# First chunk's attention units scheduled by priority, weight loads behind its stores, and a weight split with three VectorE operations and one more on ScalarE

## The chip, the cores and the metric

The kernel runs on one core of a Trainium2 chip. The metric is the time of one execution on the device, in microseconds (us). Three runs of the kernel before took 1007.69, 1010.55 and 1011.11 us; the median is 1010.55.

## The reference

Attention with a sliding window of 32 positions and 32 global tokens per batch, then a feed-forward layer with a residual. There are 8 batches, 8 heads, 512 local positions, 32 global ones and a head size of 64; all is float32.

```
s_ll = where(|i - j| <= 32, scale * q_l @ k_l.T, -1e9)      # local rows
s_l  = concat([scale * q_l @ k_g.T, s_ll]);  out_l = softmax(s_l) @ concat([v_g, v_l])
out_g = softmax(scale * q_g @ concat([k_g, k_l]).T) @ concat([v_g, v_l])
x   = concat([out_g, out_l])  as (8, 576, 512)
xn  = (x - mean) / sqrt(var + 1e-6) * g_ln
out = x + relu(xn @ w_ch1) @ w_ch2                          # 512 -> 2048 -> 512
```

## The kernel before

**Units and chunks.** A `Local` unit is one batch, one pair of heads and 256 positions. Its `scores` (L249) are TensorE's score matmuls (L262), VectorE's minimum of each row with the mask added (L275, four per unit) and ScalarE's exponential (L285, four). `transposes` (L294) turns the probabilities, for the first 16 units on TensorE (L299) with a copy `pt` on ScalarE (L301). `values` (L309) are the value matmuls (L316), a reciprocal of the sums (L326 on GpSimd, L327) and x on VectorE (L328). After the four units of a half, `finish` stores x to DRAM (L342, two stores on SP's queue) and `norm` takes its statistics (L189, L191 on VectorE, L193 and L194 on GpSimd) and normalises: by ScalarE (L202), or, for the last half of the first chunk, by VectorE into a new tile (L207). `transpose_chunk` (L484) turns x into the feed-forward's operand: a transpose on TensorE (L492), its high part `xh` on ScalarE (L504) and the rest `xl` on VectorE (L505).

A chunk is 512 rows. There are eight chunks of eight units each and one of the global rows. `ffn` runs a chunk through 16 slices of the weights: `mm1` (L531, 12 matmuls of 512 columns), ScalarE's `hh` (L539), VectorE's `hl` (L540) and `mm2` (L550, 12 matmuls, one slice behind). The units of the next chunk are dealt out among the slices.

**Weights.** Each slice arrives as 1024 packed 64-bit words per partition (`raw`, loaded at L165, 1 MB). In the first chunk `split_weights` (L133) makes a high and a low float32r part of each: ScalarE's L140, VectorE's L142 and L143, L145 and L146, ScalarE's cast L150, VectorE's L152. L145 and L146 are the last readers of `raw`. The buffers of raw words borrow the places of late weight slices (`RAWS`, L27): four for the first eight loads, then fewer, so a load waits until an earlier slice has been split. `tmp` has two buffers.

**Order.** Each engine runs its instructions in one order, and an instruction that waits holds what stands behind it. The block at L685 to L726 handles the first chunk's eight units (`need[0]` is 8, `HP` is 4). It runs under `manual_schedule` for SP, TensorE, VectorE and ScalarE: on these engines the order is that of the Python code. The code deals out one step of a weight split between the steps of the units from the fourth on (`SPLIT_FROM`). Loads of weights stand among those of the units (L690, L691). From L733 on TensorE alone has the written order; for the other engines a scheduler orders by its own estimate of times and by priority (`hurry` is `tc.high_priority()`).

Of the kernel before, what the change touches and what calls it, by code (L numbers as in the profile page):

```python
# [11 lines left out]
I32 = mybir.dt.int32  # L12
I16 = mybir.dt.int16
U16 = mybir.dt.uint16
# [3 lines left out]
ALU = mybir.AluOpType  # L18
# [8 lines left out]
RAWS = ("w15", "w14", "w13", "ob", "w15", "w14", "w13", "ob") + ("w15", "w14", "ob") * 2 + ("w15", "ob")  # L27
UNITS = ("w5", "w6", "w7", "w8", "w9", "w10", "w11", "w12")


SPLIT_AHEAD = 3
LOADS_AHEAD = 2
SPLIT_FROM = 3

ON_PE = 16

# [12 lines left out]
def attention_ffn_kernel(  # L49
# [33 lines left out]
    def f32(ap):  # L83
        return ap.bitcast(F32)
# [48 lines left out]
    def split_weights(ap, raw, hi, lo):  # L133

        third = raw.bitcast(U16).rearrange("p (n t) -> p n t", t=4)[:, :, 1]
        top = raw.bitcast(I32).rearrange("p (n t) -> p n t", t=2)[:, :, 1]
        tmp = ap.tile([P, KT * P + DM], F32, name="tmp", bufs=2)
        itmp = tmp.bitcast(I32)
        last = tmp.bitcast(U16).rearrange("p (n t) -> p n t", t=2)[:, :, 0]
        nc.scalar.activation(tmp, f32(top), AF.Abs, scale=REBIAS)  # L140
        yield
        nc.vector.tensor_scalar(tmp, tmp, HUGE, None, ALU.min)  # L142
        nc.vector.tensor_scalar(itmp, itmp, 3, None, ALU.logical_shift_left)  # L143
        yield
        nc.vector.scalar_tensor_tensor(last, third, THIRD, last, ALU.mult, ALU.add)  # L145
        nc.vector.scalar_tensor_tensor(  # L146
            itmp, top, SIGN, itmp, ALU.bitwise_and, ALU.bitwise_or
        )
        yield
        nc.scalar.copy(hi, tmp)  # L150
        yield
        nc.vector.tensor_tensor(lo, tmp, f32(hi), op=ALU.subtract)  # L152
# [67 lines left out]
    class Local:  # L220
# [88 lines left out]
        def values(self):  # L309
            b, hp, half = self.at  # L310
            pv = self.bank(3, "pv")
            for h in range(2):
                for qb in range(2):
                    for g in range(4):
                        gp = slice(g * WIN, (g + 1) * WIN)
                        nc.tensor.matmul(  # L316
                            pv[gp, qb * P + h * D:qb * P + h * D + D],
                            self.pt[:, 2 * h + qb, gp],
                            self.v[:, 4 * qb + g, h * D:(h + 1) * D],
                            start=True,  # L320
                            stop=True,
                            tile_position=(0, g * WIN),
                            skip_group_check=True,
                        )
            ri = small.tile([P, 4], F32, name="ri")
            nc.gpsimd.tensor_scalar(ri, self.sm, SUM_EPS, None, ALU.add)  # L326
            nc.vector.reciprocal(ri, ri)  # L327
            nc.vector.tensor_tensor(  # L328
                self.x[:, :, hp * P:(hp + 1) * P].rearrange("p q (h d) -> p q h d", h=2),
                pv[:, :256].rearrange("p (q h d) -> p q h d", q=2, h=2),  # L330
                ri.rearrange("p (h q) -> p q h", h=2).unsqueeze(3).to_broadcast([P, 2, 2, D]),
                op=ALU.mult,
            )
            if not self.alone and self.next and self.next.next:
                self.next.next.load()
# [346 lines left out]

    ET = mybir.EngineType
    xt = []
    with tc.manual_schedule(engines={ET.SP, ET.PE, ET.DVE, ET.Activation}):  # L685
        begin(0)
        nc.sync.dma_start(g_sb, g_ln.rearrange("(t p) o -> p (t o)", p=P))
        for n in range(2, need[0]):
            units[n].load()
            load_weights_to((n - 1) // 2)  # L690
        load_weights_to(4)  # L691
        units[need[0]].load()
        units[need[0] + 1].load()
        splits = weights_to(SPLIT_AHEAD)
        scores = [u.scores() for u in units[:need[0]]]
        moves = {}
        after = {}
        next(scores[0])
        for n in range(need[0] + 2):
            if n < need[0]:  # L700
                for _ in scores[n]:
                    pass
            if n + 1 < need[0]:
                next(scores[n + 1])
            if 0 <= n - 1 < need[0]:
                moves[n - 1] = units[n - 1].transposes()
                next(moves[n - 1])
            if n > SPLIT_FROM:
                next(splits, None)
            if 0 <= n - 1 < need[0]:  # L710
                for _ in moves[n - 1]:
                    pass
            if n >= 2:
                after[n - 2] = values(units[n - 2])
            if n >= SPLIT_FROM:
                next(splits, None)
            if n == HP + 2:
                for _ in after[HP - 1]:
                    pass
            if n == HP + 3:  # L720
                for _ in transpose_chunk(tiles_of(ready[0][:1]), xt, 0, 4):
                    pass
        for _ in after[need[0] - 1]:
            pass
        for _ in transpose_chunk(tiles_of([units[need[0] - 1].xn]), xt, 2, 4):
            pass  # L726
    for _ in splits:
        pass
    ready.pop(0)
    traced["units"] = need[0]  # L730
    for c, chunk in enumerate(chunks):
# [119 lines left out]
```

## Time and profile before

| | |
|---|---|
| median of three runs | 1010.55 us |
| the profiled execution | 1013.72 us |
| its span | 1011.9 us |
| busy: TensorE, VectorE, ScalarE, GpSimd | 950.4, 588.1, 299.0, 44.5 us |
| chain of waits, by engine | TensorE 85%, VectorE 7%, ScalarE 2%, DMA 2%, issue 2% |

Times in a timeline count from the start of the span. The profile gives each group of instructions the line that recorded it, so the two kernels have different line numbers at the top: a split's L140, L142, L143, L145 are now L138, L139, L141, L142, while L146 to L152 and all from there up to L681 are the same in both. A matmul's listed duration includes its passage through the array, so start to start is the time it takes from the next. Durations on VectorE and ScalarE overlap in the same way by a little.

### The profile page before, as it was taken

The page shows a single profiled execution, that of the slowest core. Times are in us where ns is not written, and L with a number is a line of the kernel's source. Part 1 is how long each engine was busy: PE and PEld are TensorE (multiplying, and loading weights), DVE is VectorE, ACT ScalarE, POOL GpSimd, SP SyncE. Part 2 cuts the span into 40 slices and gives each one's busy share as a digit, 9 for nine tenths or more (in the row PEclk, how much of TensorE's full clock was granted, in tenths as well). Part 3 has the DMA queues.
Part 4 walks back from the last instruction along what each step waited for, and adds up shares of the span by engine and source line. Part 5 has one row for each costly group of instructions (what it writes and reads, how often), then busy time and mean ns, then how long its engine had stood idle before and what let it go on. Part 6 is the DMA issues. An engine that isn't in the chain of part 4 may idle for free.

```text
span 1011.9 us, 21071 instructions
## 1 busy us (share of the span) xinstructions
PE 950.4 (94%) x8616; PEld 719.4 (71%) x8616; DVE 588.1 (58%) x1889; ACT 299.0 (30%) x826; POOL 44.5 (4%) x150
## 2 busy tenths in 40 slices
PE   5429999999999999999999999999999989989997
PEld 3216777677777777777777777777777766766796
DVE  2699952567667666666667666767666632222311
ACT  5545542322232223222222223222212232222210
POOL 3010000000000000000000000000000000000000
PEclk9859999999999999999999999999999999999999
DMA  9645542232233222322232224212322344543110
GB/s 363 254 146 198 202 162 90 84 105 90 70 131 113 90 71 91 123 90 100 80 131 91 70 90 154 91 70 90 119 81 87 110 159 147 186 140 133 32 42 21
DMA packets 31872, 118.80 MB, mean 117 GB/s; under 512 B 4256, under 2 KB 6304, under 8 KB 27680
## 3 DMA queue, kind: packets, MB, share of 16 engines
q1 hardware_dynamic: 31776, 117.46, 33.8%
q8 instruction: 68, 1.11, 0.4%
q14 instruction: 28, 0.23, 0.1%
HBM read 99.62 MB, written 17.83 MB: 116 GB/s over the span
## 4 chain that ended last, share of the span: by engine, by line
PE 85%; DVE 7%; ACT 2%; DMA 2%; issue 2%; POOL 1%; SPq 0%; ACTq 0%; DVEq 0%
PE acc L550 36%; PE ph L531 36%; PE sc L262 5%; PE pv L316 3%; DVE tmp L145 2%; PE t L492 1%; PE pv L419 1%; DVE w L152 1%; DVE tmp L146 1%; ACT p L285 1%; PE sc L371 1%; DMA u<-in_eu 1%; PE tp L299 1%; DVE hl L540 1%; PE t L407 1%
## 5 line engine op out<-in xcount | busy, mean ns | idle before, releaser
L550 PE MATMUL acc<-w,hh 128*128 128x512 f32 x1088 | 344.3, 398 | 0.0
L531 PE MATMUL ph<-xh,w 128*128 128x512 f32 (+1 forms) x1216 | 311.8, 383 | 0.0
L307 DVE STREAM_TRANSPOSE pt<-p 32x128 f32<-32x128 f32 x768 | 232.6, 303 | 62.5 <-ACT p L285 50.4
L531 PEld LDWEIGHTS ph<-xh,w 128*128 128x128 f32 x1216 | 214.0, 189 | 49.8 <-issue 3.1
L550 PEld LDWEIGHTS acc<-w,hh 128*128 128x128 f32 x1088 | 206.7, 190 | 44.8
L550 PE MATMUL acc<-w,hl 128*128 128x512 f32 x544 | 226.3, 416 | 2.2 <-DVE hl L540 2.2
L540 DVE SCALAR_TENSOR_TENSOR hl<-ph,hh 128x512 fp32r<-128x512 f32 (+1 forms) x144 | 94.3, 656 | 171.0 <-ACT hh L539 169.5
L539 ACT ACTIVATE hh<-ph 128x512 fp32r<-128x512 f32 (+1 forms) x144 | 82.2, 571 | 362.8 <-PE ph L531 361.7
L285 ACT ACTIVATE p<-p,mn 128x128 f32<-128x128 f32 x256 | 99.8, 391 | 197.9 <-DVE mn L275 197.9
L531 PE MATMUL ph<-xl,w 128*128 128x512 f32 x512 | 143.7, 402 | 0.0
L550 PEld LDWEIGHTS acc<-w,hl 128*128 128x128 f32 x544 | 102.9, 189 | 31.9 <-issue 7.0
L531 PEld LDWEIGHTS ph<-xl,w 128*128 128x128 f32 x512 | 94.3, 189 | 27.9 <-issue 6.9
L275 DVE CUSTOM_DVE_ANT_0 p<-sc,mask 128x128 f32<-128x128 f32 x256 | 58.7, 286 | 45.7 <-PE sc L262 40.0
L262 PE MATMUL sc<-u 64*32 64x128 f32 x2048 | 57.5, 295 | 23.1 <-DMA u<-in_eu 8.5
L262 PEld LDWEIGHTS sc<-u 64*32 64x32 f32 x2048 | 31.9, 112 | 52.4 <-issue 35.9
L328 DVE TENSOR_TENSOR x<-pv,ri 128x256 f32<-128x256 f32 x64 | 26.9, 420 | 60.0 <-PE pv L316 59.8
L316 PEld LDWEIGHTS pv<-u,pt 128*32 128x32 f32 x2048 | 33.9, 116 | 22.6 <-issue 21.4
L285 ACT ACTIVATION_READ_ACCUMULATOR p<-p,mn 128x1 f32 x256 | 47.8, 187 | 0.0
L316 PE MATMUL pv<-u,pt 128*32 128x64 f32 x2048 | 44.5, 232 | 0.0
L492 PE MATMUL t<-ident,x 128*128 128x128 f32 x136 | 23.1, 291 | 21.1 <-DVE x L207 13.2
L326 POOL TENSOR_SCALAR ri<-sm 128x4 f32<-128x4 f32 x64 | 16.6, 259 | 589.1 <-ACT p L285 588.6
L202 ACT ACTIVATE x<-x,rs 128x512 f32<-128x512 f32 x32 | 24.8, 810 | 43.0 <-DMA xs<-x 42.9
(58 smaller groups left out, 440.3 us busy)
## 6 DMA issues: line engine op xcount, KB each, us to landing
u<-in_eu SPq DMA_DIRECT2D x63, 848.0 KB, 4.7
raw<-in_wd SPq DMA_DIRECT2D x16, 1024.0 KB, 6.1
gk<-in_gk SPq DMA_DIRECT2D x8, 1088.0 KB, 5.1
xs<-x SPq DMA_DIRECT2D x32, 256.0 KB, 5.6
ob<-xs SPq DMA_DIRECT2D x32, 256.0 KB, 3.9
out<-ob SPq DMA_DIRECT2D x32, 256.0 KB, 2.1
gv<-in_gv SPq DMA_DIRECT2D x8, 1024.0 KB, 5.0
u<-in_eu SPq DMA_DIRECT2D x1, 512.0 KB, 3.7
```

The costliest lines, as they stand in the source:

```text
L202: nc.scalar.activation(x[:, j, :], x[:, j, :], AF.Identity, bias=rs[:, 1, j:j + 1], scale=rs[:, 0, j:j + 1],)
L262: nc.tensor.matmul(sc[h][gp, qb * P:(qb + 1) * P], self.e[hd, w * WIN:(w + 1) * WIN], self.e[hd, k0 * WIN:(k0 + 4) * WIN], start=True, sto ...
L275: nc.vector.tensor_tensor_reduce(out=self.p[:, c], in0=sc[h][:, qb * P:(qb + 1) * P], in1=masks[half, qb], scale=-QSCALE, scalar=BIG, op0= ...
L285: nc.scalar.activation(self.p[:, c], self.p[:, c], AF.Exp, bias=mn[:, c:c + 1], scale=-1.0, accum_out=self.sm[:, c:c + 1],)
L307: nc.vector.transpose(out=self.pt[rp, :, gp], in_=self.p[gp, :, rp])
L316: nc.tensor.matmul(pv[gp, qb * P + h * D:qb * P + h * D + D], self.pt[:, 2 * h + qb, gp], self.v[:, 4 * qb + g, h * D:(h + 1) * D], start= ...
L328: nc.vector.tensor_tensor(self.x[:, :, hp * P:(hp + 1) * P].rearrange("p q (h d) -> p q h d", h=2), pv[:, :256].rearrange("p (q h d) -> p ...
L492: nc.tensor.transpose(t[:, j * P:(j + 1) * P], xn[j][:, kt * P:(kt + 1) * P], ident)
L531: nc.tensor.matmul(ph[:, :n], w[:, kt, :], xx[kt][:, :n], start=(i == 0), stop=(i == 3 * KT - 1),)
L539: nc.scalar.activation(hh[:, :n], ph[:, :n], AF.Relu)
L540: nc.vector.scalar_tensor_tensor(hl[:, :n], ph[:, :n], 0.0, f32(hh[:, :n]), ALU.max, ALU.subtract)
L550: nc.tensor.matmul(acc[t], a[:, ts], w, start=(f == 0 and i == 0), stop=(f == NF - 1 and i == 2),)
```

## The change

It has three parts. In the split, VectorE's L145 goes: ScalarE scales the 16-bit field itself (new L139, into the low word of `raw`, in place) and VectorE's shift takes it in by an or (new L142, in place of L143). The first chunk's block keeps only SP in written order; the units' code stands under `hurry(True)`, and the splits come after it, without priority. And SP's order is written anew: in front of the units only slice 0 is loaded; slice 1 and two units of the next chunk are loaded behind the stores of the first half, slices 2 and 3 behind those of the second.

```
@@ -27,10 +27,8 @@
 RAWS = ("w15", "w14", "w13", "ob", "w15", "w14", "w13", "ob") + ("w15", "w14", "ob") * 2 + ("w15", "ob")
 UNITS = ("w5", "w6", "w7", "w8", "w9", "w10", "w11", "w12")
 
-
 SPLIT_AHEAD = 3
 LOADS_AHEAD = 2
-SPLIT_FROM = 3
 
 ON_PE = 16
 
@@ -136,13 +134,15 @@
         top = raw.bitcast(I32).rearrange("p (n t) -> p n t", t=2)[:, :, 1]
         tmp = ap.tile([P, KT * P + DM], F32, name="tmp", bufs=2)
         itmp = tmp.bitcast(I32)
-        last = tmp.bitcast(U16).rearrange("p (n t) -> p n t", t=2)[:, :, 0]
+        last = raw.bitcast(I32).rearrange("p (n t) -> p n t", t=2)[:, :, 0]
         nc.scalar.activation(tmp, f32(top), AF.Abs, scale=REBIAS)
+        nc.scalar.activation(last, third, AF.Copy, scale=THIRD)
         yield
         nc.vector.tensor_scalar(tmp, tmp, HUGE, None, ALU.min)
-        nc.vector.tensor_scalar(itmp, itmp, 3, None, ALU.logical_shift_left)
+        nc.vector.scalar_tensor_tensor(
+            itmp, itmp, 3, last, ALU.logical_shift_left, ALU.bitwise_or
+        )
         yield
-        nc.vector.scalar_tensor_tensor(last, third, THIRD, last, ALU.mult, ALU.add)
         nc.vector.scalar_tensor_tensor(
             itmp, top, SIGN, itmp, ALU.bitwise_and, ALU.bitwise_or
         )
@@ -682,50 +682,46 @@
 
     ET = mybir.EngineType
     xt = []
-    with tc.manual_schedule(engines={ET.SP, ET.PE, ET.DVE, ET.Activation}):
+    with tc.manual_schedule(engines={ET.SP}):
         begin(0)
         nc.sync.dma_start(g_sb, g_ln.rearrange("(t p) o -> p (t o)", p=P))
         for n in range(2, need[0]):
             units[n].load()
-            load_weights_to((n - 1) // 2)
-        load_weights_to(4)
-        units[need[0]].load()
-        units[need[0] + 1].load()
-        splits = weights_to(SPLIT_AHEAD)
-        scores = [u.scores() for u in units[:need[0]]]
-        moves = {}
-        after = {}
-        next(scores[0])
-        for n in range(need[0] + 2):
-            if n < need[0]:
-                for _ in scores[n]:
-                    pass
-            if n + 1 < need[0]:
-                next(scores[n + 1])
-            if 0 <= n - 1 < need[0]:
-                moves[n - 1] = units[n - 1].transposes()
-                next(moves[n - 1])
-            if n > SPLIT_FROM:
-                next(splits, None)
-            if 0 <= n - 1 < need[0]:
-                for _ in moves[n - 1]:
-                    pass
-            if n >= 2:
-                after[n - 2] = values(units[n - 2])
-            if n >= SPLIT_FROM:
-                next(splits, None)
-            if n == HP + 2:
-                for _ in after[HP - 1]:
-                    pass
-            if n == HP + 3:
-                for _ in transpose_chunk(tiles_of(ready[0][:1]), xt, 0, 4):
-                    pass
-        for _ in after[need[0] - 1]:
+            if n == 3:
+                load_weights_to(1)
+        with hurry(True):
+            scores = [u.scores() for u in units[:need[0]]]
+            after = {}
+            next(scores[0])
+            for n in range(need[0] + 2):
+                if n < need[0]:
+                    for _ in scores[n]:
+                        pass
+                if n + 1 < need[0]:
+                    next(scores[n + 1])
+                if 0 <= n - 1 < need[0]:
+                    for _ in units[n - 1].transposes():
+                        pass
+                if n >= 2:
+                    after[n - 2] = values(units[n - 2])
+
+                if n == HP + 1:
+                    load_weights_to(2)
+                    units[need[0]].load()
+                    units[need[0] + 1].load()
+                if n == HP + 2:
+                    for _ in after[HP - 1]:
+                        pass
+                if n == HP + 3:
+                    for _ in transpose_chunk(tiles_of(ready[0][:1]), xt, 0, 4):
+                        pass
+            load_weights_to(4)
+            for _ in after[need[0] - 1]:
+                pass
+            for _ in transpose_chunk(tiles_of([units[need[0] - 1].xn]), xt, 2, 4):
+                pass
+        for _ in weights_to(SPLIT_AHEAD):
             pass
-        for _ in transpose_chunk(tiles_of([units[need[0] - 1].xn]), xt, 2, 4):
-            pass
-    for _ in splits:
-        pass
     ready.pop(0)
     traced["units"] = need[0]
     for c, chunk in enumerate(chunks):
```

VectorE's row shows where the first split stands among the units. `mask_114` and `mask_122` mark the minima of the units of the second half, 4 to 7; `x` and `ri` belong to the unit named by its place. Before, from the middle of the first split:

```order
L142 TENSOR_SCALAR tmp<-tmp 128x1024
L143 TENSOR_SCALAR tmp<-tmp 128x1024
L327 RECIPROCAL ri<-ri 128x4
L328 TENSOR_TENSOR x<-pv,ri 128x2x128
L145 SCALAR_TENSOR_TENSOR tmp<-raw,tmp 128x1024
L146 SCALAR_TENSOR_TENSOR tmp<-raw,tmp 128x1024
L275 ISA p,mn<-sc,mask_114 128x128
L275 ISA mn 128x1
```

And now, the same stretch:

```order
L142 SCALAR_TENSOR_TENSOR tmp<-tmp,raw 128x1024
L328 TENSOR_TENSOR x<-pv,ri 128x2x128
L146 SCALAR_TENSOR_TENSOR tmp<-raw,tmp 128x1024
L327 RECIPROCAL ri<-ri 128x4
L152 TENSOR_TENSOR w<-tmp,w 128x1024
L275 ISA p,mn<-sc,mask_114 128x128
L275 ISA mn 128x1
L275 ISA p,mn<-sc,mask_122 128x128
```

Before, the split's L142 to L146 stood behind the minima of unit 4 and ahead of those of unit 5, with L152 later. Now the whole split stands ahead of the minima of unit 4, and no other split follows before unit 7's.

SP's row shows the loads (`u` of a unit, `raw` of a slice) and stores (`xs`) of the first chunk. Before:

```order
L245 DMA u<-in_eu 128x1696 x2
L165 DMA raw<-in_wd 128x1024
L245 DMA u<-in_eu 128x1696 x2
L165 DMA raw<-in_wd 128x1024
L245 DMA u<-in_eu 128x1696 x2
L165 DMA raw<-in_wd 128x1024 x2
L245 DMA u<-in_eu 128x1696 x2
L165 DMA raw<-in_wd 128x1024
L342 DMA xs<-x 128x512 x2
L165 DMA raw<-in_wd 128x1024 x3
L342 DMA xs<-x 128x512 x2
```

And now:

```order
L245 DMA u<-in_eu 128x1696 x2
L165 DMA raw<-in_wd 128x1024
L245 DMA u<-in_eu 128x1696 x4
L165 DMA raw<-in_wd 128x1024
L342 DMA xs<-x 128x512 x2
L165 DMA raw<-in_wd 128x1024
L245 DMA u<-in_eu 128x1696 x2
L165 DMA raw<-in_wd 128x1024
L342 DMA xs<-x 128x512 x2
L165 DMA raw<-in_wd 128x1024 x5
```

The first `raw` behind the four units is that of the fifth slice, which waits for the first split; those of the second, third and fourth slice moved behind stores that wait for x.

ScalarE's row shows the end of the first chunk's units, from the last unit's `pt` to the last `xh`, the operand's second half. Before:

```order
L301 COPY pt<-tp 128x512
L150 CAST w<-tmp 128x1024
L140 ACTIVATE tmp<-raw 128x1024
L150 CAST w<-tmp 128x1024
L140 ACTIVATE tmp<-raw 128x1024
L150 CAST w<-tmp 128x1024
L504 ACTIVATE xh_618<-t,g_sb 128x256 x2
L140 ACTIVATE tmp<-raw 128x1024
L504 ACTIVATE xh_630<-t,g_sb 128x256 x2
```

And now:

```order
L301 COPY pt<-tp 128x512
L139 ACTIVATE raw<-raw 128x1024
L504 ACTIVATE xh_593<-t,g_sb 128x256 x2
L138 ACTIVATE tmp<-raw 128x1024
L139 ACTIVATE raw<-raw 128x1024
L504 ACTIVATE xh_605<-t,g_sb 128x256 x2
L138 ACTIVATE tmp<-raw 128x1024
L139 ACTIVATE raw<-raw 128x1024
L150 CAST w<-tmp 128x1024
```

Casts (L150) went to later places, and the two operations on a raw slice (L138 and L139, here of the third and then the fourth slice) stand ahead of and behind the last `xh`.

## Rows read from the trace of the kernel before

**Rows 1.** The page's busy times: us (share of the span) and instructions.
```profile
PE 950.4 (94%) x8616; PEld 719.4 (71%) x8616; DVE 588.1 (58%) x1889; ACT 299.0 (30%) x826; POOL 44.5 (4%) x150
```

**Rows 2.** Windows: length; busy us of each engine; PEclk; DMA share; GB/s.
```profile
0.00:5.00 5.00, 1.11 (x32) 0.66 (x32) 0.00 (x0) 1.49 (x2) 4.06 (x24) 1.00 0.65 232
5.00:10.00 5.00, 1.23 (x32) 0.81 (x32) 1.84 (x15) 2.24 (x11) 3.90 (x19) 1.00 0.83 308
10.00:15.00 5.00, 4.12 (x72) 3.05 (x72) 1.14 (x11) 2.97 (x15) 0.22 (x1) 1.00 1.01 427
```

**Rows 3.** Timeline of TensorE: start, us, line, operation [idle before <- releaser].
```profile
17.43 1.57 PE L262 MATMUL sc<-u 64*32 64x128 f32 x32 [1.01 <-DVE mn L275]
18.93 1.11 PE L299 MATMUL tp<-ident,p 128*128 128x128 f32 x4
19.98 1.08 PE L316 MATMUL pv<-u,pt 128*32 128x64 f32 x32
...
67.76 1.27 PE L492 MATMUL t<-ident,x 128*128 128x128 f32 x4 [13.19 <-DVE x L207]
...
75.99 2.07 PE L531 MATMUL ph<-xh,w 128*128 128x512 f32 x4
...
100.27 0.67 PE L262 MATMUL sc<-u 64*32 64x128 f32 x32
...
189.62 1.20 PE L531 MATMUL ph<-xh,w 128*128 128x512 f32 x4
```

**Rows 4.** Timeline of VectorE, around the splits and the second statistics.
```profile
28.57 0.28 DVE L275 CUSTOM_DVE_ANT_0 p<-sc,mask 128x128 f32<-128x128 f32 x1
...
35.98 0.16 DVE L196 SCALAR_TENSOR_TENSOR rs<-mv,rs 128x2 f32<-128x2 f32 x1 [1.15 <-POOL rs L194]
...
57.60 1.23 DVE L152 TENSOR_TENSOR w<-tmp,w 128x1024 fp32r<-128x1024 f32 x1
58.73 1.24 DVE L146 SCALAR_TENSOR_TENSOR tmp<-raw,tmp 128x1024 int32<-128x1024 int32 x1
...
60.66 0.41 DVE L328 TENSOR_TENSOR x<-pv,ri 128x256 f32<-128x256 f32 x1
61.00 0.68 DVE L143 TENSOR_SCALAR tmp<-tmp 128x1024 int32<-128x1024 int32 x1
61.60 1.28 DVE L189 BATCH_NORM_STATS2 st<-x 128x6 f32<-128x512 f32 x2
62.79 1.28 DVE L145 SCALAR_TENSOR_TENSOR tmp<-raw,tmp 128x1024 uint16<-128x1024 uint16 x1
...
67.07 1.00 DVE L207 TENSOR_SCALAR x<-x,mv,rs 128x512 f32<-128x512 f32 x2 [0.63 <-POOL rs L194]
...
70.33 0.86 DVE L505 SCALAR_TENSOR_TENSOR xl<-t,g_sb,xh 128x256 fp32r<-128x256 f32 x2
```

**Rows 5.** Timeline of ScalarE.
```profile
40.93 1.52 ACT L202 ACTIVATE x<-x,rs 128x512 f32<-128x512 f32 x2
...
44.55 0.40 ACT L285 ACTIVATE p<-p,mn 128x128 f32<-128x128 f32 x1 [2.10 <-DVE mn L275]
...
46.10 1.03 ACT L150 CAST w<-tmp 128x1024 fp32r<-128x1024 f32 x1
47.04 0.57 ACT L301 COPY pt<-tp 128x512 f32<-128x512 f32 x1
47.52 1.15 ACT L140 ACTIVATE tmp<-raw 128x1024 f32<-128x1024 f32 x1
48.56 0.82 ACT L504 ACTIVATE xh<-t,g_sb 128x256 fp32r<-128x256 f32 x2
...
128.21 1.14 ACT L140 ACTIVATE tmp<-raw 128x1024 f32<-128x1024 f32 x1 [5.32 <-DMA raw<-in_wd]
```

**Rows 6.** SP's timeline; then DMA issues of 40 to 140 us: KB, us to landing.
```profile
33.32 1.56 SPq L342 DMA_DIRECT2D xs<-x  x2
...
raw<-in_wd SPq DMA_DIRECT2D x11, 1024.0 KB, 4.8
```

## Prediction, as put on record before the run

> **What bounds the kernel now.** I read the page first: TensorE is busy for 94% of the span [rows 1]. Then the windows and TensorE's timeline, to find where it is not at work. The first feed-forward matmul starts at 75.99 us, and the one that opens the second chunk at 189.62 [rows 3]; behind that the chain of waits is TensorE's nearly throughout. So the end moves by what moves TensorE through the first chunk: A, the time until the first feed-forward matmul, and B, the 113.6 us from there to 189.62.
>
> In A nothing is full. TensorE's last long wait before it, 13.19 us, is for VectorE's normalised tile (L207) of the second half [rows 3]; VectorE was at weight splits between the units' small operations, as at 57.60 to 62.79 [rows 4]. The eight units' own work is short, so A is a chain of waits and an order question. The clock: the window of 10 to 15 us reads 1.00 [rows 2], but 32 score matmuls take 1.57 us at 17.43 and 0.67 at 100.27 [rows 3]. I take the durations: 1.2 GHz in the early stretch, 2.4 GHz later.
>
> **Prices.** On VectorE and ScalarE listed durations overlap the next by about 0.09 us (57.60 + 1.23 against 58.73), so I take that off. VectorE [rows 4]: row minima of a unit 0.84 (four of 0.21), x 0.34, two statistics 1.19, L143 0.60, L145 1.18, L146 1.14, L152 1.13, two normalisations (L207) 1.0, two xl 0.8. ScalarE [rows 5]: four exponentials 1.55, the pt copy 0.48, L140 1.04, the cast L150 0.94, two xh 0.73, two L202 1.43. TensorE at the low level [rows 3]: scores 1.5, transposes 1.05, values 1.06. A reciprocal, a pair of aggregates or a hand-over between engines is put at 0.1.
>
> **The split.** Before, VectorE works 0.60 + 0.60 + 1.18 + 1.14 + 1.13 = 4.65 us on one slice. L145 goes; L143 becomes an operation on two tensors. No row shows that one: at least the 0.60 of L143, at most the 1.18 of L145; I take L146's 1.14, which reads the same kinds. New: 0.60 + 1.14 + 1.14 + 1.13 = 4.0, so 0.65 less (0.6 to 1.2). ScalarE gains L139 with 16-bit input: not below the cast's 0.94, not above the 1.18 that VectorE needs for these operands; I take L140's 1.04, so its slice costs 1.04 + 1.04 + 0.94 = 3.0. Over 16 slices VectorE gives up 10 us and ScalarE takes 17, but neither is on the path once TensorE is fed (B, below).
>
> **A: the order.** Before, VectorE ends five splits in A and is in the sixth, the first two between the units' steps. Now it ends one ahead of unit 4's minima, one behind unit 7's transposes, and part of two more at the end. I walk the new order, each engine in its row; SP's and ScalarE's orders are the two that new waits come from, GpSimd's changes only among masks and small additions.
> - To 17.0. Loads decide, as before. The first slice's raw stands behind four units' loads: 4.5 MB, which the 232, 308 and 427 GB/s of the first windows [rows 2] deliver by 14.3. ScalarE has some 0.6 of unit 2's exponentials and a copy ahead then, and goes on with L138 and L139: 17.0.
> - To 21.8. L142 1.14, x 0.34, L146 1.14, ScalarE's cast 0.94, L152 1.13, hand-overs 0.1: the split is done at 21.8. Scores of unit 4 were there at 18.6, so this first split costs the units 3.2. Minima 22.6, exponentials 23.7, copy 24.1.
> - To 28.5. ScalarE's next instruction is L139 of the fifth slice, whose load was issued when L146 freed its buffer (19.7) and stands behind units 4 to 7: 9.0 MB, at 425 GB/s landed at 25.0. It ends at 26.1, 2.0 late. Unit 5's exponentials end at 27.7; TensorE meanwhile does scores 6, and x of unit 3 is written at 28.5.
> - To 45.0. Statistics to 29.8, the hand-over to GpSimd and back 1.15 [rows 4], L202 to 32.6, unit 7's exponentials 34.2, a copy 34.7. Slice 1's load is issued behind two stores of x, 1.56 of issue [rows 6], at 30.2. A load issued alone lands in 4.8 [rows 6], with the stores' 0.5 MB in front (1.2 at 425 GB/s) 6.0: 36.2. L138 and L139 38.3, L142 39.4, x 39.8, xl 40.6; two transposes and xh 41.5, xl 42.0, unit 7's transposes 43.1, copy 43.6, values and x 45.0.
> - To 57.5. Two chains start from that x. One: statistics and aggregates 46.4, GpSimd 47.5, L207, transposes, xh: 50.0. The other: two stores 1.6, slice 2's load 5.4 (half the stores' 1.2 added): 52.0. On ScalarE L138 and L139 of slice 2 stand ahead of the last two xh: 54.1, xh 54.9, VectorE's L142 55.2, xl 56.0; unit 8's scores need the banks that this frees: 57.5.
>
> That makes the first feed-forward matmul 57.5; hand-overs that I dropped are put at 0.5: 58.0. A is shorter by 76.0 - 58.0 = 18.0. About 2 of what remains is the load behind the stores. The bounds of the two unknown prices move A by -1.6 to +0.1 (three L142 on the path) and by -0.4 to +0.6 (four L139).
>
> **B: is it still fed?** From unit 8's scores on TensorE's order is the same as before. At the start of B it has two slices split and a third under way, where before five were and a sixth under way. VectorE has 14 left: 14 x 4.0 + 16 hl of 0.6 + 8 units of 1.3 = 76 us, less than the 113.6 of B (before 10 x 4.65 + 9.6 + 10.4 = 67). ScalarE's 17 more lie beside these matmuls too. ScalarE has 3.0 + 0.5 + half a unit (1.0) = 4.5 a slice against TensorE's 113.6 / 16 = 7.1. But L139 of a later slice stands ahead of nearer casts and relus, and ScalarE waits in order for its load: walked through, that holds it 0.4 to 1.3 us a slice, and once (the tenth load) TensorE stands 2.2. Before has stalls of its own in B, about as much. I put B at no change, bounded by -3 and +5. SP's later stores stand ahead of the last load, which is needed 20 us later: nothing.
>
> **Sum.** The profiled execution is 1013.72 us, 1.8 around its span; less 18.0 makes 995.7. The median of the runs shown is 1010.55, 3.2 below the profiled one, so I expect 992.5.
>
> **Rivals.**
> 1. *TensorE wakes in the units.* In my walk it works from 10.9 to 21.1 almost without a gap, where before it was busy 4.12 of 5 us and stayed low [rows 2, 3]. At 2.4 GHz scores, transposes and values go from 3.6 to 1.6 a unit. Along the chain some four such steps of 0.5 to 1.0 and the last scores (0.9) come out, 4 us: 988. Against: the chain is held by ScalarE and loads, and narrow matmuls did not lift the clock before. The Trainium skill (TensorE: Matmul & The Clock Gate, Part 1) says half rate is the default and sustained activity releases it. By that rule this rival holds; the trace so far, with the score rows, speaks for the low level.
> 2. *The units come out slower than walked.* The loads that ScalarE waits for in A (first, second, third and fifth slice) each land later, 1.5 to 2.5 us, because unit loads share the engines; A ends at 66: 8 to 10 us gained, 1001. For it: ScalarE once stood 5.32 for a load [rows 5]. Against: later loads were issued into a quieter queue.
> 3. *Slower.* ScalarE's L139 waits in B become the bound. A slice has 7.1 - 4.5 = 2.6 us to spare; to lose the 18 won, 14 slices must each take 2.6 + 18 / 14 = 3.9 of waiting. If every load held ScalarE for its 4.8, a slice would be 9.3: 14 x 2.2 = 31 lost, less 18: 1023. Against: the loads are issued three slices ahead.
> 4. *The order does not matter:* VectorE's postponed splits (four more of 4.0 at the start of B) hold TensorE by just what A gave, 16 to 18: 1010.
>
> **Chances.** Forecast (987 to 998) 0.62, rival 1 0.12, rival 2 0.17, rival 3 0.06, rival 4 0.03. Range 985 to 1003. About 0.3% (3 us) is what can be told from no change: faster 0.91, same 0.03, slower 0.06.
>
> **What will show it.** The first L531 at 55 to 61 us; no split operation on VectorE between the first L152, at about 22, and about 38; L139 near 1.05 and L142 near 1.2 in the list; ScalarE idle for raw before L139 at about 24; SP's third load behind the second pair of stores; the 113.6 of B within 5. Wrong if the first L531 comes after 68, or if TensorE in B waits for hl or a weight for more than 6 us in all.

## The result and the profile after

The changed kernel took 995.42, 997.54 and 999.27 us against a median of 1009.63 us for the kernel before, a ratio of 0.988 (95% interval 0.9847 to 0.9914). A fourth run, of 4931.53 us, was disturbed and is left out. A second measurement, with six runs, gave 0.9867 (0.9835 to 0.9899). So the change is worth some 12 to 13 us; 18 were forecast. The page, where [rows 1] stood:

```profile
PE 948.8 (95%) x8616; PEld 717.2 (72%) x8616; DVE 578.0 (58%) x1873; ACT 314.7 (32%) x842; POOL 44.0 (4%) x150
```

VectorE does 10 us less and ScalarE 16 more, as the prices said. The first feed-forward matmul and the start of chunk 2, 75.99 and 189.62 in [rows 3], are now in TensorE's timeline (start, us, operation, idle before and its releaser):

```profile
20.90 0.66 PE L299 MATMUL tp<-ident,p 128*128 128x128 f32 x4
...
51.12 1.09 PE L492 MATMUL t<-ident,x 128*128 128x128 f32 x4 [3.88 <-DVE x L207]
...
59.53 2.00 PE L531 MATMUL ph<-xh,w 128*128 128x512 f32 x4
...
64.88 0.33 PE L299 MATMUL tp<-ident,p 128*128 128x128 f32 x1 [1.15 <-ACT p L285]
...
106.09 0.65 PE L316 MATMUL pv<-u,pt 128*32 128x64 f32 x32 [0.51 <-ACT pt L301]
...
122.91 1.10 PE L262 MATMUL sc<-u 64*32 64x128 f32 x30 [1.27 <-DVE x L328]
...
176.91 1.20 PE L531 MATMUL ph<-xh,w 128*128 128x512 f32 x4
...
873.47 1.05 PE L371 MATMUL sc<-gk,gq 64*32 64x272 f32 x16 [1.31 <-DVE gp L381]
```

A is 59.53, B is 176.91 - 59.53 = 117.4. The wait of 13.19 for L207 is 3.88. Between 60 and 125 us there are nine short waits that add up to 5.8 us, 3.4 of it for ScalarE's p and pt; before, four that add up to 2.6. At 122.91 thirty score matmuls take 1.10 where 0.67 was usual: during the wait before them the granted clock had dropped to half for a moment. The window of 120 to 130 us shows it (columns as in [rows 2]: the third number from the end is the granted clock, 1.00 in this window of the kernel before):

```profile
120.00:130.00 10.00, 8.73 (x89) 6.36 (x78) 9.49 (x19) 6.89 (x14) 0.51 (x1) 0.83 0.53 190
```

ScalarE, where [rows 5] stood. Each bracket that ends in "DMA raw" is ScalarE standing still for a slice that has not landed:

```profile
27.57 1.10 ACT L139 ACTIVATE raw<-raw 128x1024 int32<-128x1024 uint16 x1 [2.34 <-DMA raw<-in_wd]
...
54.26 1.12 ACT L138 ACTIVATE tmp<-raw 128x1024 f32<-128x1024 f32 x1 [1.39 <-DMA raw<-in_wd]
55.27 1.12 ACT L139 ACTIVATE raw<-raw 128x1024 int32<-128x1024 uint16 x1
56.29 0.83 ACT L504 ACTIVATE xh<-t,g_sb 128x256 fp32r<-128x256 f32 x2
...
104.40 1.17 ACT L139 ACTIVATE raw<-raw 128x1024 int32<-128x1024 uint16 x1 [2.46 <-DMA raw<-in_wd]
105.45 0.59 ACT L301 COPY pt<-tp 128x512 f32<-128x512 f32 x1
```

The last two rows are the pattern of B: L139 waits for a load, the copy pt stands behind it, and TensorE at 106.09 waits for pt. The group of L139 over the whole span (busy, mean ns, idle before and releaser):

```profile
L139 ACT ACTIVATE raw<-raw 128x1024 int32<-128x1024 uint16 x16 | 18.5, 1156 | 10.7 <-DMA raw<-in_wd 10.7
```

VectorE, where [rows 4] stood; after the first L152 the next operation of a split comes at 39.34:

```profile
21.58 1.23 DVE L152 TENSOR_TENSOR w<-tmp,w 128x1024 fp32r<-128x1024 f32 x1 [0.82 <-ACT w L150]
...
39.34 0.69 DVE L141 TENSOR_SCALAR tmp<-tmp 128x1024 f32<-128x1024 f32 x1 [1.00 <-ACT tmp L138]
```

SP, where [rows 6] stood, with the loads behind each pair of stores:

```profile
20.54 0.33 SPq L165 DMA_DIRECT2D raw<-in_wd  x1
31.90 0.81 SPq L342 DMA_DIRECT2D xs<-x  x2
32.75 0.46 SPq L165 DMA_DIRECT2D raw<-in_wd  x1
...
47.76 0.80 SPq L342 DMA_DIRECT2D xs<-x  x2
48.60 11.37 SPq L165 DMA_DIRECT2D raw<-in_wd  x3
```

### The profile page after: what moved, and what is told of

The parts are those of the page before. It is cut to its first block, busy times and chain, and to the rows that moved or that the text cites. A ratio compares the mean times of both kernels' runs of the same rounds, so it can differ in the third digit from the quotient of the medians.

```text
span 993.6 us, 21066 instructions
## 1 busy us (share of the span) xinstructions
PE 948.8 (95%) x8616; PEld 717.2 (72%) x8616; DVE 578.0 (58%) x1873; ACT 314.7 (32%) x842; POOL 44.0 (4%) x150
## 4 chain that ended last, share of the span: by engine, by line
PE 85%; DMA 3%; DVE 3%; ACT 2%; issue 1%; SPq 0%; POOL 0%; ACTq 0%; DVEq 0%
PE acc L550 37%; PE ph L531 36%; PE sc L262 4%; PE pv L316 3%; DMA raw<-in_wd 2%; PE t L492 1%; PE pv L419 1%; DMA xs<-x 1%; PE sc L371 1%; PE t L407 1%; DVE tmp L142 0%; DVE hl L540 0%; DVE pt L307 0%; DVE tmp L146 0%; ACT p L285 0%
## 5 line engine op out<-in xcount | busy, mean ns | idle before, releaser
L531 PE MATMUL ph<-xh,w 128*128 128x512 f32 (+1 forms) x1216 | 311.7, 382 | 0.0
L531 PEld LDWEIGHTS ph<-xh,w 128*128 128x128 f32 x1216 | 214.0, 188 | 49.8 <-issue 3.1
L531 PE MATMUL ph<-xl,w 128*128 128x512 f32 x512 | 143.4, 401 | 0.0
L531 PEld LDWEIGHTS ph<-xl,w 128*128 128x128 f32 x512 | 94.0, 188 | 27.8 <-issue 6.9
L262 PEld LDWEIGHTS sc<-u 64*32 64x32 f32 x2048 | 32.3, 112 | 41.6 <-issue 25.1
L202 ACT ACTIVATE x<-x,rs 128x512 f32<-128x512 f32 x32 | 24.8, 811 | 45.1 <-DMA xs<-x 43.5
```

What stands on the lines that cost most here:

```text
L202: nc.scalar.activation(x[:, j, :], x[:, j, :], AF.Identity, bias=rs[:, 1, j:j + 1], scale=rs[:, 0, j:j + 1],)
L262: nc.tensor.matmul(sc[h][gp, qb * P:(qb + 1) * P], self.e[hd, w * WIN:(w + 1) * WIN], self.e[hd, k0 * WIN:(k0 + 4) * WIN], start=True, sto ...
L531: nc.tensor.matmul(ph[:, :n], w[:, kt, :], xx[kt][:, :n], start=(i == 0), stop=(i == 3 * KT - 1),)
```

## The experiments

Each was timed beside the kernel before. The changed kernel without the priority (hurry(False) around the units) was not run: its program is the same as that of the changed kernel, instruction for instruction on all five engines, so the priority in the diff does nothing.

The table is from the profiles, one execution each: A until the first feed-forward matmul, B from there to chunk 2, the start of chunk 2, and the rest of the span. Line numbers shift by a few between the kernels.

| kernel | A | B | chunk 2 at | rest | ratio to before (95%) |
|---|---|---|---|---|---|
| before | 75.99 | 113.63 | 189.62 | 822.3 | 1 |
| changed | 59.53 | 117.38 | 176.91 | 816.7 | 0.988 (0.9847 to 0.9914) |
| after_again | 60.14 | 118.97 | 179.11 | 821.7 | 0.9867 (0.9835 to 0.9899) |
| split_only | 73.53 | 119.81 | 193.34 | 816.8 | 1.0042 (1.0018 to 1.0065) |
| order_only | 56.27 | 115.83 | 172.10 | 820.6 | 0.9831 (0.9800 to 0.9862) |
| early_loads | 73.17 | 113.30 | 186.47 | 817.3 | 0.9984 (0.9962 to 1.0007) |
| later_one | 51.83 | 121.07 | 172.90 | 817.7 | 0.9834 (0.9807 to 0.9861) |
| earlier_one | 56.85 | 113.59 | 170.44 | 818.1 | 0.9835 (0.9811 to 0.9860) |
| later_new | 57.16 | 115.08 | 172.24 | 816.9 | 0.9848 (0.9825 to 0.9870) |
| pool139 | 63.81 | 121.38 | 185.19 | 821.4 | 0.9975 (0.9956 to 0.9993) |
| mixed_late7 | 51.42 | 122.82 | 174.24 | 818.4 | 0.9862 (0.9827 to 0.9897) |
| mixed_late | 51.80 | 123.71 | 175.51 | 818.5 | 0.9866 (0.9836 to 0.9896) |

TensorE's clock has a part in these columns. In some executions it falls to half for a while in B or in the rest, mostly at a wait or just behind one. The next table has, for B, TensorE's idle waits, what is left of B without them, and how long TensorE's granted clock stood at 1.2 GHz, the start of B included (us):

| profile | waits in B | B without them | at 1.2 GHz in B |
|---|---|---|---|
| before | 2.6 | 111.0 | 2.6 |
| changed | 5.8 | 111.6 | 5.2 |
| order_only | 3.7 | 112.1 | 7.1 |
| split_only | 6.8 | 113.1 | 7.6 |
| later_one | 6.7 | 114.4 | 9.7 |
| after_again | 4.9 | 114.0 | 11.6 |

So a wait can cost more than its own length. The rest, where the edits change no work, is 816.7 to 817.3 in the four profiles in which the clock does not fall there before the last few us, 817.7 to 818.5 in the four in which it falls early in chunk 2, 820.6 in order_only, where it falls in the global rows, and 821.4 to 822.3 in the three in which it falls in both places.

**after_again**: the changed kernel, unedited.

> The changed kernel once more, beside the others and with more rounds. Its first profile gave three differences to the kernel before: 16.5 us less until the first feed-forward matmul (A), 3.8 more in the first chunk of the feed-forward (B), and 5.6 less behind it, where no instruction moved. If those 5.6 belong to the change, the time is again some 18 below the kernel before and the profile shows again fewer waits in the last stretch; if they are one execution's luck, it is 16.5 - 3.8 = 12.7 below, a ratio of 0.987 to 0.988, and the last stretch is as long as before.

The rest came out at 821.7, as long as before, so the 5.6 us that the first profile had less there were one execution's luck. The two profiles of the changed kernel differ by 5.0 us in the rest. Of that 1.9 is one wait in the global rows: ScalarE's L202 stands for a store of x, 7.22 us in the first profile and 9.11 here, and what stands behind it in order passes this on to TensorE, which waits 3.20 here and 1.31 in the first profile, at 873.47. The first line is from the first profile:

```profile
871.04 0.82 ACT L202 ACTIVATE x<-x,rs 128x512 f32<-128x512 f32 x1 [7.22 <-DMA xs<-x]
```
```profile
876.66 0.81 ACT L202 ACTIVATE x<-x,rs 128x512 f32<-128x512 f32 x1 [9.11 <-DMA xs<-x]
...
879.09 1.05 PE L371 MATMUL sc<-gk,gq 64*32 64x272 f32 x16 [3.20 <-DVE gp L381]
```

The other 3.1 us come with the clock: the same matmuls at half rate for a while. Here the granted clock falls behind that wait and early in chunk 2; in the first profile it reads 1.00 in both windows (185 to 195 and 880 to 885 us):

```profile
185.00:195.00 10.00, 7.81 (x84) 5.74 (x85) 3.87 (x16) 1.06 (x4) 0.00 (x0) 0.83 0.31 99
880.00:885.00 5.00, 5.00 (x26) 4.05 (x20) 1.52 (x7) 2.05 (x5) 0.22 (x1) 0.66 0.67 236
```

What the change does is in A and B: 10.5 to 12.7 us together, beside 12 to 13 by the medians.

**split_only**: the kernel before with the new split.

```
-        last = tmp.bitcast(U16).rearrange("p (n t) -> p n t", t=2)[:, :, 0]
+        last = raw.bitcast(I32).rearrange("p (n t) -> p n t", t=2)[:, :, 0]
+        nc.scalar.activation(last, third, AF.Copy, scale=THIRD)
-        nc.vector.tensor_scalar(itmp, itmp, 3, None, ALU.logical_shift_left)
+        nc.vector.scalar_tensor_tensor(itmp, itmp, 3, last, ALU.logical_shift_left, ALU.bitwise_or)
-        nc.vector.scalar_tensor_tensor(last, third, THIRD, last, ALU.mult, ALU.add)
```

> The kernel before with the new split alone; order and loads are as before. If the gain is one of order (my theory), the split brings what VectorE saves on the path of A: five splits at 0.65 less are 3.2 us, so A is near 73 and the time some 3 below before (ratio 0.997), and B is unchanged, since VectorE has spare time there. If the cheaper split makes the gain (rival), A falls by 10 or more and the ratio is 0.99 or below. If ScalarE's L139 costs as much on the path as VectorE saves, the time is that of before.

A fell by 2.5, near the 3.2 expected. But B rose by 6.2, and the kernel is slower by 0.4%. TensorE's timeline, and ScalarE's and TensorE's waits (us, times, longest; the new operation is L141 here):

```profile
73.53 2.08 PE L533 MATMUL ph<-xh,w 128*128 128x512 f32 x4
...
193.34 1.20 PE L533 MATMUL ph<-xh,w 128*128 128x512 f32 x4
```
```profile
ACT raw L141 <- DMA raw<-in_wd: 13.1, 8, 4.3
```
```profile
PE pv L318 <- ACT pt L303: 4.5, 3, 2.1
```

ScalarE stands 13.1 us for loads at the new operation, eight times, five of them (10.4 us) in A. In B TensorE stands 4.5 us for copies on ScalarE, where before it stood for none; each of the three copies stands behind operations of a split of which the first had waited for its load. Of B's 6.2 us, 4.1 are more waits of TensorE; the other 2.1 stand beside 5 us more at half clock. The split gained nothing by itself; it cost.

**order_only**: the changed kernel with the old split (the diff above, backwards).

> The changed kernel with the old split: no L139 on ScalarE, 0.65 us more on VectorE per slice. My theory (order makes the gain) has A at least as short as in the changed kernel: L139 of the fifth slice held ScalarE 2.3 us for its load and took 1.0, and the third slice's L139 another 1.0 ahead of the last xh, against two to three splits that are 0.65 longer: A 56 to 59. For B two theories part: if ScalarE's waits for loads made the 3.8 us more, B falls back to about 114 and the kernel is 3 to 6 us faster than the changed one; if VectorE is full in B's first 70 us (it is 94% busy there), 14 splits at 0.65 more add up to 9 us of work there, B is 120 or more and the kernel is 2 to 6 us slower than the changed one. The rival that the cheaper split makes the gain says 1008 and above.

```profile
56.27 2.08 PE L529 MATMUL ph<-xh,w 128*128 128x512 f32 x4
...
68.65 0.66 PE L260 MATMUL sc<-u 64*32 64x128 f32 x30 [2.00 <-DVE x L326]
...
119.53 0.67 PE L260 MATMUL sc<-u 64*32 64x128 f32 x30 [1.69 <-DVE x L326]
...
172.10 1.20 PE L529 MATMUL ph<-xh,w 128*128 128x512 f32 x4
```

A is 3.3 to 3.9 shorter than in the two profiles of the changed kernel and B 1.5 to 3.1, although VectorE has 0.65 us more per slice. So of the two theories on B the one of ScalarE's waits came out: TensorE no longer waits for p or pt in B. VectorE being fuller bit too, but less: TensorE's only two waits in B, 3.7 us together, are for VectorE's x. The median is 994.15 against 997.99 in the same session; with six runs of each that difference is at the edge of the noise. Order and loads alone give at least all of the gain. One wait for a load is left in front of the last xh, now by L138:

```profile
52.55 1.12 ACT L138 ACTIVATE tmp<-raw 128x1024 f32<-128x1024 f32 x1 [3.22 <-DMA raw<-in_wd]
53.58 0.83 ACT L502 ACTIVATE xh<-t,g_sb 128x256 fp32r<-128x256 f32 x2
```

**early_loads**: the changed kernel with the weight loads, and the two loads for units of the next chunk, ahead of the stores.

```
+        load_weights_to(4)
+        units[need[0]].load()
+        units[need[0] + 1].load()
         with hurry(True):
...
-                    load_weights_to(2)
-                    units[need[0]].load()
-                    units[need[0] + 1].load()
...
-            load_weights_to(4)
```

> The changed kernel with its weight loads put back where they were, right behind the units' loads and ahead of the stores. The prediction had the load behind the stores as a cost of about 2 us in A: by that this kernel is 2 us faster than the changed one. The rival that the order now suggests: the late loads are what keeps the splits out of the units. With the early loads VectorE has eight splits and the start of a ninth in front of the last xl, where the changed kernel has two and a start; six more at 4.0 us are 24 us of work, of which about 11 to 14 fit into VectorE's idle time between 23 and 58 us. So A gets 10 to 13 us longer (69 to 73), B gets back its 3.8, and the kernel is 6 to 10 us slower than the changed one, that is a ratio to before of 0.995 or so.

This is the run that decides. Moving the loads back takes away nearly the whole gain: ratio 0.9984, A 73.17, inside the 69 to 73 of the rival but for 0.2, and B is back at 113.30. The kernel is 11.6 us slower than the changed one, more than the 6 to 10 expected. TensorE, then VectorE in front of it:

```profile
65.06 1.08 PE L492 MATMUL t<-ident,x 128*128 128x128 f32 x4 [9.36 <-DVE x L207]
...
73.17 2.07 PE L531 MATMUL ph<-xh,w 128*128 128x512 f32 x4
```
```profile
56.74 0.42 DVE L328 TENSOR_TENSOR x<-pv,ri 128x256 f32<-128x256 f32 x1
57.07 1.22 DVE L152 TENSOR_TENSOR w<-tmp,w 128x1024 fp32r<-128x1024 f32 x1
58.20 1.22 DVE L146 SCALAR_TENSOR_TENSOR tmp<-raw,tmp 128x1024 int32<-128x1024 int32 x1
59.34 1.28 DVE L189 BATCH_NORM_STATS2 st<-x 128x6 f32<-128x512 f32 x2
```

The last unit's x comes at 56.74 (47.30 in the changed kernel) and its statistics stand behind two more operations of splits: the picture of [rows 4], with the scheduler's order in place. Eight splits end on VectorE before the last xl; in the changed kernel two do, before five. The scheduler put the split of a slice that is loaded early into VectorE's row among the units; the late load is what keeps it away. Late loads under the written order of the kernel before were not run, so it is not shown that they would do as much without the scheduler.

**later_one** and **earlier_one**: order_only with one slice less, or one more, loaded behind the first stores.

```
later_one:
-                    load_weights_to(2)
earlier_one:
-                    load_weights_to(2)
+                    load_weights_to(3)
```

> The old split and the new order, with slice 1's load moved behind the second pair of stores too, so that one split (not two) stands in front of the last xl, and a second in part. If late loads are what keeps splits off the path of A, A gets shorter again: in the kernel with two splits (A 56.3) slice 1's split stood among the last units' steps, and ScalarE held the last xh 3.2 us for slice 2's load. Here x of the last unit comes some 4 us earlier and its stores and the load behind them too, so A is 51 to 53. B has one split more to do, and VectorE is busy for 19 of 20 us there: it grows by 0 (if the splits are off TensorE's path) to 4.7 (if one split's time comes straight back). So 0 to 4 us faster than 994. If the gate theory is wrong, A stays at 56.

> The old split and the new order, with slice 2's load moved ahead, beside slice 1's behind the first stores. Now three splits stand in front of the last xl, and ScalarE no longer has to wait 3.2 us for slice 2's load in front of the last xh. By the gate theory each split let into A costs up to its 4.65 us there, less what falls into VectorE's idle time: A 57 to 60 against 56.3, B about 1 less: 0 to 3 us slower than 994. By the prediction's view, in which the load behind the stores was a cost, A gets 2 to 3 shorter and the kernel 2 to 4 faster.

```profile
51.83 2.07 PE L529 MATMUL ph<-xh,w 128*128 128x512 f32 x4
...
64.81 1.02 PE L260 MATMUL sc<-u 64*32 64x128 f32 x30 [2.01 <-DVE x L326]
...
172.90 1.20 PE L529 MATMUL ph<-xh,w 128*128 128x512 f32 x4
```
```profile
56.85 2.07 PE L529 MATMUL ph<-xh,w 128*128 128x512 f32 x4
...
170.44 1.20 PE L529 MATMUL ph<-xh,w 128*128 128x512 f32 x4
```

The first fence is later_one, the second earlier_one. In later_one A fell by 4.4, and B rose by 5.2: the split taken out of A came straight back, beyond the 4.7 that were expected at most. In earlier_one A rose by only 0.6 and B fell by 2.2. Neither view had that: by the view that each split let into A lengthens it, a third costs 1 to 4, by the prediction's view A gets shorter. The third split in A was almost free, as ScalarE no longer waits for a load ahead of the last xh; so the number of splits in A does not set A by itself. Medians are 991.52 and 990.90, ratios like order_only's. Both beat the kernel before. Each of the three ratios overlaps with the changed kernel's; taken together, and each run set against the kernel before of its session, their 17 runs lie 1.4 to 6.1 us below the changed kernel's nine (an estimate from the recorded times). Which of the three is best can't be told.

**later_new**: the changed kernel with the edit of later_one, the new split kept.

> The changed kernel, new split and all, with slice 1's load moved behind the second pair of stores. If L139 costs what it did between the changed kernel and the one with the old split (3.3 in A by ScalarE's waits for loads and by its own 1.04, 1.5 in B), this is 3 to 5 us slower than the same order with the old split, and 0 to 4 faster than the changed kernel. If VectorE's fuller row decides when one split more is left for B, the cheaper split now pays and this one is the faster of the two.

```profile
52.90 1.14 ACT L139 ACTIVATE raw<-raw 128x1024 int32<-128x1024 uint16 x1
53.91 0.85 ACT L504 ACTIVATE xh<-t,g_sb 128x256 fp32r<-128x256 f32 x2
```

A is 57.16, 5.3 more than with the old split, and B 6.0 less; chunk 2 starts at the same time, and the medians (994.60 against 991.52) can't be told apart with four and six runs. In A L139 costs more than the 3.3 expected; the fence shows it ahead of the last xh. In B the cheaper split looked as if it paid, which the next two tested.

**mixed_late7** and **mixed_late**: later_one with the new split from slice 7, or slice 5, on.

```
+FIRST_NEW = 7
...
-        nc.scalar.activation(last, third, AF.Copy, scale=THIRD)
+        if f >= FIRST_NEW:
+            nc.scalar.activation(last, third, AF.Copy, scale=THIRD)
...
+        if f < FIRST_NEW:
+            nc.vector.scalar_tensor_tensor(last, third, THIRD, last, ALU.mult, ALU.add)
```

> Late loads as in later_one, with the old split for slices 0 to 6 and the new one from slice 7 on. The runs so far say that L139 costs where ScalarE's row holds the units of A (later_new: A 57.2, with the old split 51.8) and that the cheaper split pays where VectorE is full, in B (115.1 against 121.1). If both are right, this has A at 51 to 53 and B at 116 to 119 (nine slices at 0.65 less are 5.9 us of VectorE's row, of which some falls behind the stretch that stalls), so chunk 2 starts at 168 to 171 and the time is 1 to 4 us below later_one's. If B's length is not VectorE's work but the late start of the first slices, B stays at 121.

> The same with the new split from slice 5 on. Two more slices at 0.65 less on VectorE, early in B where it stalls: B 1 us shorter than with slice 7. Against: L139 of slices 5 and 6 stands early in B ahead of a relu or an exponential, and its loads are issued when slices 1 and 2 are split, so ScalarE may wait 1 to 3 us there as it did for L139 in the changed kernel; then B is 1 to 3 us longer than with slice 7. A 51 to 53 in both.

A came out as expected, 51.42 and 51.80. B did not fall: 122.82 and 123.71. With A at 51 to 52 it is 121 to 124 whatever the split, with A at 56 to 57 it is 114 to 116. In mixed_late7 TensorE, and then ScalarE, show that two things offset each other:

```profile
64.39 1.10 PE L272 MATMUL sc<-u 64*32 64x128 f32 x30 [1.98 <-DVE x L338]
...
115.83 0.33 PE L309 MATMUL tp<-ident,p 128*128 128x128 f32 x1 [2.13 <-ACT p L295]
```
```profile
114.26 1.13 ACT L144 ACTIVATE raw<-raw 128x1024 int32<-128x1024 uint16 x1 [2.60 <-DMA raw<-in_wd]
```

The first wait is later_one's of 64.81: x stands behind splits in VectorE's row, which is busy for 29.4 of the 30 us from 60 to 90. TensorE's waits for x in B fall from 6.0 us in later_one to 4.4. But the new split's operation on ScalarE (L144 here) waits for its load again, p stands behind it, and TensorE's waits for ScalarE, none in later_one, come to 2.5. So these runs do not show that VectorE's work is without effect on B; they show that the new split gains nothing there either. What sets the sum of A and B, 170 to 176 us in all kernels with late loads and the old split at the start, was not settled; the clock, at half for 12.1 and 12.8 us of B in these two, is a part of it.

**pool139**: the changed kernel with L139 on GpSimd.

```
-        nc.scalar.activation(last, third, AF.Copy, scale=THIRD)
+        nc.gpsimd.tensor_scalar(last, third, THIRD, None, ALU.mult)
```

> The changed kernel with L139 on GpSimd in place of ScalarE: VectorE keeps the cheap split, ScalarE's row is again that of the old split. If it is ScalarE's place that made L139 dear (it stands in order ahead of exponentials, xh and relus and waits for a load there), A and B come out as with the old split or better: A 55 to 58, B 114 to 116, a time of 990 to 995. If GpSimd takes so long over 1024 elements (its small operations go from 0.2 to 1.1 us beside VectorE) that VectorE's L142 waits for it, or slows VectorE down, splits come late and the time is 1000 or more.

The second case came. GpSimd takes 3.1 us for it, and VectorE's L141 grows beside it. First GpSimd's group over the span, then VectorE's of L141 between 60 and 130 us, here and in the changed kernel:

```profile
L139 POOL TENSOR_SCALAR raw<-raw 128x1024 int32<-128x1024 uint16 x16 | 49.8, 3113 | 51.7 <-DMA raw<-in_wd 36.6 <-ACT pt L301 7.2 <-DVE mn L275 4.9
```
```profile
L141 DVE TENSOR_SCALAR tmp<-tmp 128x1024 f32<-128x1024 f32 x12 | 12.4, 1036 | 0.1
```
```profile
L141 DVE TENSOR_SCALAR tmp<-tmp 128x1024 f32<-128x1024 f32 x13 | 8.9, 685 | 1.7 <-ACT tmp L138 1.7
```

L141 takes 1.04 instead of 0.69. The Trainium skill (SBUF — State Buffer, "Who interferes with whom") says that VectorE, in the modes that use two ports, and GpSimd lock each other out of a shared pair of ports, and that whoever comes second is fully blocked for the whole instruction. The longer L141 agrees with it in kind; but of the sixteen L141, five take 1.36 to 1.63 and the others 0.68 or 0.69, five of these wholly inside one of GpSimd's operations of some 3 us, so a block for the whole instruction is not what this run shows. The run doesn't tell what L139 off ScalarE is worth by itself: A rose to 63.81, as GpSimd is slow, L141 grows, and slice 2's load landed 1.9 us later than in the changed kernel.

## Why the prediction was right, and where it was off

**A.** Forecast 58.0, measured 59.53 and 60.14. The execution fell behind the walk mostly at one place, the fifth slice:

| station of the walk | forecast | measured |
|---|---|---|
| split 0 done | 21.8 | 22.7 |
| L139 of the fifth slice ends | 26.1 | 28.6 |
| x of unit 3 | 28.5 | 31.8 |
| x of unit 7 | 45.0 | 47.6 |
| slice 2 landed (L138 starts) | 52.0 | 54.3 |
| last xl done | 56.0 | 58.3 |
| first L531 | 58.0 | 59.5 |

The term that was mis-sized is ScalarE's wait for the fifth slice: it was put at 2.0 us, L139 with it, and cost 3.4 (from the end of the copy at 25.1), since the load was issued 0.8 later and took 7.0 us, not 5.3. Another 0.8 came by the x of unit 3, ahead of which the next unit's minima stand on VectorE; later steps took less than the walk gave them. The late fifth slice is rival 2's mechanism at a quarter of its size or less. Nearly all prices held: L142 1.14 from start to start (1.14 taken), L139 1.0 (1.04 taken). In the list, with the overlap, L139 is 1.16 and not near 1.05.

**B.** "I put B at no change" failed by 3.8 and 5.3 us, the second beyond its bound of +5. The walk saw L139 ahead of nearer work, 0.4 to 1.3 us of waiting a slice, and set this against stalls of the kernel before of about the same size. TensorE's own stalls were 2.6 us before and are 5.8 now (4.9 in the second profile), and it stands at half clock longer, which the prediction did not put into B. Ruling out harm by an average (4.5 of ScalarE's 7.1 us a slice) was the mistake: an engine with a third of its time to spare still makes TensorE wait if its order puts a wait for a load in front of pt. That is rival 3 in kind, at a sixth of its price or less. split_only shows it alone: B +6.2.

**The split.** "Over 16 slices VectorE gives up 10 us and ScalarE takes 17, but neither is on the path once TensorE is fed (B, below)." In B ScalarE's part was on it: with the old split B is 1.5 to 3.1 shorter. In A, where the walk had both, VectorE's part is worth 2.5 in the order of the kernel before (split_only), and in the new order ScalarE's costs more than that: with the old split A is 3.3 to 3.9 shorter (order_only).

**The load behind the stores.** The prediction counted it as a cost: "About 2 of what remains is the load behind the stores." In early_loads the same loads moved ahead make A 13 to 14 us longer. Under the scheduler's order it is the cause of the gain, and the prediction, which read the new order off the engines' rows, did not see what made that order. Its A was right because the rows were right. The priority that the diff adds does nothing here.

**The sum.** 16.5 gained in A (15.9 in the second profile), 3.8 given back in B (5.3), so 10.5 to 12.7; the forecast of 18 lacks 1.5 to 2.1 in A and the whole of B. The profiled execution came to 995.42, beside the forecast 995.7, by the luck of 5.6 in the rest; the medians are the measure, 997.54 and 997.99 against the forecast 992.5.

**The other rivals.** Rival 1: TensorE did wake in the units. Four transposes take 0.66 us at 20.90 and 1.12 at 44.31; at 20.90 TensorE had worked almost without a gap since 11.0. The Trainium skill (TensorE: Matmul & The Clock Gate, Part 1) says that activity releases the half rate; the row at 20.90 agrees. But after ScalarE's wait at 27.57 the clock fell again (the granted clock is 0.50 throughout 38 to 61 us), and A was no shorter, since the chain ran over ScalarE and the loads. The prediction's ground against this rival, that narrow matmuls did not lift the clock before, was a misreading. In the kernel before they did, later in A:

```profile
39.29 1.12 PE L299 MATMUL tp<-ident,p 128*128 128x128 f32 x4
...
41.22 0.66 PE L299 MATMUL tp<-ident,p 128*128 128x128 f32 x4
```

Rival 4 (order does not matter) fails for the change, but later_one is its case: what is taken out of A below 56 or so comes back in B there.

**What was to be seen.** First L531 inside 55 to 61; no split between 21.58 and 39.34; ScalarE idle for raw from about 25 to 27.57; SP's third load behind the second stores: all as put. B within 5: 3.8 once, 5.3 once. TensorE waited 2.9 us for hl in the first 300 us, 2.2 of it in chunk 2, under the 6 named.

## What to carry to other kernels

Where a scheduler fills an engine's row with whatever has its data, the time of a load decides the order, so test a change of order and a change of loads apart; a load put later can be worth more than a priority. An operation moved to an engine with time to spare still costs if it waits there, in order, for a transfer: look at what stands behind it, not at the engine's busy share. And changes that come together may have opposite signs: here the late loads gave 12 us (early_loads against the changed kernel) and the split took some of it back (3.5 in split_only, some 4 between order_only and the changed kernel). An idle wait also has a second price where the clock falls behind it.

## What was not expected of the hardware

- The same instruction of the global rows, in an unchanged stretch, waited 1.31 us in one profile of the changed kernel and 3.20 in the other (3.46 before, 3.58 in order_only), as a store of x landed later. The clock fell behind this wait in the four profiles in which it took 3.06 to 3.58 us, and not in the eight in which it took 0.82 to 1.58; wait and clock together make most of the 5 us by which two profiles of one kernel differ behind the change. So the stretch that the change touches has to be compared by itself.
- Two queued loads of the same 1 MB took different times beside other traffic: the fifth slice, behind the units' loads, 7.0 us from issue (20.54) to ScalarE's start (27.57), against the 4.8 of [rows 6].
- ScalarE's L139, 16-bit input with a stride and a 32-bit result in place, takes 1.16 us on average for 1024 elements, about the same as L138 with 32-bit words (1.15); GpSimd takes 3.1 for it.
